# A retention layer and a feed-forward layer on one core: when the weight forms are stored, when GpSimd scales a unit's q, and where the masks of the scores stand

## The chip, the cores and the metric

The kernel runs on one core of a Trainium2 chip. The metric is the device time of one execution in microseconds. Three executions of the kernel before took 833.71, 831.45 and 833.17 us; the median is 833.17.

A core has five engines, each with an instruction order of its own: TensorE (PE; PEld is its loading of weights), VectorE (DVE), ScalarE (ACT), GpSimd (POOL) and SyncE (SP), which only issues DMAs. ScalarE and GpSimd issue DMAs too. Every engine works its instructions off in order: an instruction that waits holds up everything behind it on that engine.

## The reference

```python
def _attn_ref(q, k, v):                      # 8 x 8 x 576 x 64, float32
    scores = np.matmul(q, k.transpose(0, 1, 3, 2)) / np.sqrt(64)
    gamma = 1.0 - 2.0 ** (-5.0 - np.arange(H))
    rel = pos[:, None] - pos[None, :]
    Dmat = np.where(rel >= 0, gamma[:, None, None] ** rel[None, :, :], 0.0)
    return np.matmul(scores * Dmat[None], v)

def _moe_ref(x, w1, w2, w3, w_out):          # x: 4608 x 512
    a = x @ w1                               # 512 x 1024
    b = x @ w2                               # 512 x 1024
    h = a * b @ w3                           # 1024 x 1024
    return h @ w_out                         # 1024 x 512
```

The attention's output, with the heads laid side by side, is x (4608 tokens by 512). All is float32.

## The kernel before, in words

**Attention** runs in 20 units g: four pairs of batches, and in each pair five stretches of the sequence (64, 128, 128, 128 and 128 positions). A unit's q is scaled by a decay, its v by another; k and q are transposed; `score(g)` multiplies them (L233) into four PSUM banks and VectorE multiplies these by a mask into `pm` (L236, four instructions); `pv_state` and `pv` (L274, L299) make the output of the unit, which ScalarE copies to the token tiles `xT` (L306); `state` (L255) carries the sum over k and v to the next unit. In units 5 to 9 and from 12 on, q, and in some of these k, is loaded in blocks of 32 (`load_blocks`, L171, 16 DMAs for a tensor of 128 positions, on SP's queue), scaled on GpSimd for q (`scale_blocks`, L181, one instruction for each of the two batches) and transposed by VectorE (`front_blocks`, L190).

**Feed-forward.** The products are Strassen-Winograd products: seven block products P1 to P7 in place of eight, of weight forms (A11, A12, S3, A22, S1, S4, S2) with token forms (B11 and so on). W3 times W_out is multiplied first (w3o). An `up` step makes x times w1 and w2 for one of 12 tiles of 384 tokens and a quarter of the hidden columns (seven products, L528): VectorE adds five of them up in a tile `c` (`plus`, L533), ScalarE copies the sixth (L546, L561), and VectorE multiplies both halves of `c` into `ab` (L566). A `down` step takes pairs of 128-token tiles of `ab` through w3o (L651) to the output, with sums on VectorE (L614, L618, L620, L699, L701, L655).

**Two levels.** For the last eight token tiles, in four groups of two (`ready` says at which units a new group starts), `up2` steps make two levels of Strassen (L1068), 14 to a group, h = 0 and 1 with seven outer products each. Their weights are the outer forms of the weight forms. `weight_forms(h, second)` makes them in place in wA[h] and wS[h] with four sums, each of two VectorE instructions (L891), and stores each form in DRAM (`kept`); `next_forms` loads them from there one outer product at a time into a ring of three tiles `ra` (L969), issued on GpSimd. The stores of the first sum's results and of the parts that take no sum go out on GpSimd's queue; those of the other sums on SP's.

Inside a step of `up2`, GpSimd adds some of the tiles `cc` up (L1073), VectorE does it for results that come from PSUM (L1078, L1080). Completed results wait in a list; `multiply(n)` takes n off it and multiplies the two halves into `ab` (L1040, both inputs in SBUF). `finish()` runs what the last step left behind.

**The order around the change.** It is written out by hand. `todo` holds the steps to come; `work(n)` runs n of them and, after each, the small entries that follow it. `aside`, `spread`, `beside` and `loads` hold closures which the steps call at fixed places: each `plus` of an `up` step takes one from `aside` and one from `spread`. So an entry in `spread` that does nothing moves the next ones by one sum. `flush` runs all that is left in `spread`. In units 6 to 9 of the first loop, the `up` steps of token tile (1, 0) run between the attention units, with the weight forms spread between their sums: the first two `up` steps use wA[0], and after them the forms of h = 0 may overwrite it.

In the last loop `dealt` says how many steps each unit takes (3, 4, 4, 3, 3, 7, 7, 3, 7, 7 for units 10 to 19), and `tail` how many of them come after the transposes. A unit runs: the first steps, the scaling of the next unit's v and q, two steps with the transposes of q and k, the tail, `pv(g)`, the multiplications if a group ends, `state(g + 1)` and `score(g + 1)`, the next group's steps.

Of the kernel before, what the change touches and what calls it, by code (L numbers as in the profile page):

```python
# [13 lines left out]
ALU = mybir.AluOpType  # L14
# [5 lines left out]
def kernel(  # L20
# [20 lines left out]
    P = 128  # L41
# [16 lines left out]
    QC = CV // 2  # L58
# [64 lines left out]
    for c in (0, slice(1, NC)):  # L123
        n = short if c == 0 else P
# [11 lines left out]
    wA = [wp.tile([P, 2, 2, KD // 2, CV], F32, tag=f"wA{h}", name="wA") for h in halves]  # L136
# [35 lines left out]
                                      src[a, :, s0:s0 + BL, f * BL:(f + 1) * BL].rearrange("m r x -> r m x"))  # L172
        live["bl_" + nm, g] = t

    def scale_blocks(g):
        c = g % NC
        n, n0 = sizes[c] // BL, starts[c] // BL
        t = live["bl_q", g]
        for b in range(2):
            part = t[:, b * NP:(b + 1) * NP, :n, :]  # L180
            nc.gpsimd.tensor_tensor(  # L181
                out=part, in0=part, in1=gqs[:, :, n0:n0 + n].unsqueeze(3).to_broadcast([P, NP, n, BL]),
                op=ALU.mult)
# [388 lines left out]
    aside, owed, spread, beside, loads = [], [], [], [], []  # L572
    g = 0
# [306 lines left out]
    def weight_forms(h, second):  # L880

        engine = nc.sync if second else nc.gpsimd

        wa, ws = wA[h].rearrange("p r j c n -> p (r j) c n"), wS[h]

        def tt(out, in0, in1, op):
            def both():
                for w in (wa, ws):
                    o, x, y = (w[:, :, c, m * QC:(m + 1) * QC] if w is wa else w[:, :, m, :, c, :]
                               for m, c in (out, in0, in1))  # L890
                    nc.vector.tensor_tensor(out=o, in0=x, in1=y, op=op)  # L891
            return both

        def send(pieces):
            for lo, m, c in pieces:
                if m == 1 and c is not None and lo < 12 * P:
                    place = kept[h][:, :, 4 * P:8 * P].rearrange("a p (j c n) -> a p j c n", j=2, c=2)[:, :, :, c]
                    for a in range(4):
                        f, r = divmod(a, 2)
                        engine.dma_start(place[a], wA[h][:, r, :, c, m * QC + f * P:m * QC + f * P + P])  # L900
                    for j in range(2):
                        engine.dma_start(place[4:7, :, j].rearrange("a p n -> p a n"), wS[h][:, :, m, j, c, :])
                    continue
                n = 2 * P if c == 1 else 4 * P
                for a in range(4):
                    f, r = divmod(a, 2)
                    x = wA[h][:, r, :, :, m * QC + f * P:m * QC + f * P + P]
                    x = x.rearrange("p j c n -> p (j c) n") if c is None else x[:, :, c, :]
                    engine.dma_start(kept[h][a, :, lo:lo + n].rearrange("p (g n) -> p g n", n=P), x)
                to = kept[h][4:7, :, lo:lo + n].rearrange("a p n -> p a n")  # L910
                if c is None:
                    engine.dma_start(to, wS[h][:, :, m].rearrange("p a j c n -> p a (j c n)"))
                else:
                    for j in range(2):
                        engine.dma_start(to[:, :, j * P:(j + 1) * P], wS[h][:, :, m, j, c, :])

        if second:
            return [tt((1, 1), (1, 1), (1, 0), ALU.subtract), tt((0, 0), (1, 1), (0, 0), ALU.add),
                    tt((0, 1), (0, 1), (1, 1), ALU.subtract),
                    lambda: send([(8 * P, 0, None), (12 * P, 1, 1)])]  # L920
        return [tt((1, 0), (0, 0), (1, 0), ALU.subtract), lambda: send([(4 * P, 1, 0)]),
                lambda: send([(0, 0, None), (5 * P, 1, 1)])]

    def weight_of(slot, nm, w):
        lo = {"A11": 0, "A12": P, "S3": 4 * P, "A22": 5 * P, "S1": 8 * P, "S4": 9 * P, "S2": 12 * P}[nm]
# [212 lines left out]
    def add_group(gr):  # L1138
        X, Y = groups[gr]
        todo.extend((up2, gr, n) for n in range(14))  # L1140
        todo.extend([(down, (X, 0), (X, 1)), (down, (X, 2), (Y, 2)), (down, (Y, 0), (Y, 1))])

    def work(n):
        while n > 0 and todo:
            fn, *args = todo.pop(0)

            nxt = next((x for x in todo if x[0] in real), None)
            if nxt and nxt[0] is down:
                if fn is down:
                    args.append(nxt[1:])  # L1150
                else:
                    ahead(*nxt[1:], 1 if fn is up2 else 3)
            if g == G and not todo:
                fn(*args, last=True)
            else:
                fn(*args)
            n -= 1
            while todo and todo[0][0] not in real:
                todo.pop(0)[0]()
# [11 lines left out]
    for g in first_pair:  # L1171
        n = (1, 1, 2, 2)[g - NC]
        if not in_blocks[g + 2]:
            load(g + 2, "k")
            load_blocks(g + 2, "q")
        scale(g + 1, "v")
        if not in_blocks[g + 1]:
            front(g + 1, "k")
            front_blocks(g + 1, "q")
        half = (n + 1) // 2  # L1180
        if in_blocks[g + 1]:
            scale_blocks(g + 1)
            work(n - 1)
            aside.extend([lambda: front_blocks(g + 1, "q"), lambda: None, lambda: front_blocks(g + 1, "k")])
            work(1)
            while aside:
                aside.pop(0)()
            half = 0
        if in_blocks[g + 2] and g + 2 < 2 * NC:
            load_blocks(g + 2, "q")  # L1190
            load_blocks(g + 2, "k")
        work(half)
        if g < NC + 2:

            weight_forms(g - NC, False)[2]()
        pv(g)()
        load(g + 2, "v", nc.scalar if in_blocks[g + 2] else nc.sync)
        if in_blocks[g + 2] and (g + 2) % NC != NC - 1:
            load(g + 2, "k")
        state(g + 1)  # L1200
        score(g + 1)
        if not in_blocks[g + 2]:
            scale_blocks(g + 2)
        if g == NC + 1:
            list(strassen_tokens(1, 0))
            forms = [(lambda h=h, second=second: spread.extend(weight_forms(h, second)[:None if second else 2]),)
                     for h in halves for second in (False, True)]
            ups = [(up, 1, 0, fp) for fp in range(NQ)]
            later = (lambda: spread.append(lambda: None),)
            todo.extend([*ups[:2], forms[0], later, forms[1], ups[2], ups[3], (flush,), forms[2], (flush,), (down, (1, 0), (1, 1)),  # L1210
                         (down, (2, 2), (3, 2)), (open_second,), (down, (3, 0), (3, 1))])
        if not in_blocks[g + 1]:
            work(n // 2)
# [27 lines left out]
    for g in range(2 * NC, G):  # L1241
        n = dealt[g - 2 * NC]
        if g + 1 < G:
            q_blocks = g > 2 * NC
            if not q_blocks:
                beside.extend(lambda j=j: scale(g + 1, "q", range(j, j + H // 2)) for j in (0, H // 2))
            tail = {3: 0, 4: 1, 7: 3}[n]
            work(n - 2 - tail)
            beside.extend(lambda j=j: scale(g + 1, "v", range(j, j + H // 2)) for j in (0, H // 2))
            if q_blocks:  # L1250
                scale_blocks(g + 1)
            for nm in "qk":
                blocks_in = q_blocks if nm == "q" else g + 1 not in whole
                if blocks_in:
                    aside.append(lambda nm=nm: front_blocks(g + 1, nm))
                work(1)
                while aside:
                    aside.pop(0)()
                if not blocks_in and nm == "k":
                    while loads:  # L1260
                        loads.pop(0)()
                    front(g + 1, "k" if q_blocks else "kq")
                if g + 2 < G and not (nm == "k" and g + 2 in whole):
                    load_blocks(g + 2, nm)
            work(tail)
            for left in (loads, beside):
                while left:
                    left.pop(0)()
        else:
            work(n)  # L1270
        pv(g)()
        if g in ready:
            finish()
            multiply()
        if g + 2 < G:
            load(g + 2, "v", nc.gpsimd)
            if (g + 2) % NC != NC - 1:
                loads.append(lambda g=g: load(g + 2, "k", nc.gpsimd))
        if g + 1 < G:
            state(g + 1)  # L1280
            score(g + 1)
        if g in ready:
            add_group(ready[g])
            token_forms(ready[g])
    g = G
# [44 lines left out]
```

## Time and profile before

The profile was taken of the execution of 833.71 us. Its span, from the first to the last instruction, is 832.0 us, so 1.71 us lie around it.

| | us |
|---|---|
| time, median of three executions | 833.17 |
| time of the profiled execution | 833.71 |
| its span | 832.0 |
| TensorE's waits at 0 to 80 us of the span | 8.0 |
| TensorE's busy time from 80 to 304 us | 223.6 of 224 |
| TensorE's busy time from 304 to 320 us | 13.94 of 16 |
| TensorE's busy time from 320 to 816 us | 493.1 of 496 |
| VectorE's 64 multiplications L1040, median and longest of one | 0.549 and 3.267 |
| stores of weight forms on GpSimd's queue: wA in 256 KB, wA in 128 KB, wS in 768 KB, wS in 192 KB | 8, 16, 2 and 8 DMAs |

A timeline line of the profile has the start and the length in us, the engine, the line of the kernel, the operation, what it writes and reads, the shape, how many instructions were merged, and in brackets how long the engine idled before and what ended that. SPq, ACTq and POOL with DMA_DIRECT2D are DMAs being issued. A line of a table of stretches has the stretch, its length, busy time and number of instructions, the granted clock of TensorE (1.00 is full speed), the busy share of the DMA engines and GB/s.

### The profile page before, as it was taken

To read this page: it belongs to the slowest core of one execution; us is meant where nothing else is said; L and a number is where in the kernel's file an instruction comes from. 1 tells how busy PE (TensorE), PEld (TensorE's weight loads), DVE (VectorE), ACT (ScalarE), POOL (GpSimd) and SP (SyncE) were. 2 spreads that over 40 slices of the span, in tenths; PEclk is the share of its full clock that TensorE was granted. 3 is DMA by queue.
4 is the path that set the end of the run, shared out by engine and by line. 5 is a ranking of instruction groups with operands and counts; after the bars stand their busy time and mean duration, and the time that the engine had idled before them with its cause. 6 is when DMAs were issued, how large, how long until landed. Compare 5 with 4: busy or idle time off the path is not lost.

```text
span 832.0 us, 15840 instructions
## 1 busy us (share of the span) xinstructions
PE 815.6 (98%) x6117; PEld 735.6 (88%) x6117; DVE 546.6 (66%) x962; ACT 291.6 (35%) x609; POOL 233.6 (28%) x272
## 2 busy tenths in 40 slices
PE   7899999999999999999999999999999999999998
PEld 7889999744888998889999889998889998899987
DVE  4899999992553576754557655677745667646653
ACT  4787566581111111245443024341034331033300
POOL 1000000001506342125556005565006460045600
PEclk9999999999999999999999999999999999999999
DMA  9995464446347659667886447978245453046401
GB/s 191 228 224 133 78 152 128 120 109 110 137 79 218 124 115 267 212 181 202 195 227 186 97 86 208 237 224 220 54 94 180 158 196 115 35 149 213 142 26 51
DMA packets 197036, 126.96 MB, mean 153 GB/s; under 512 B 158072, under 2 KB 178680, under 8 KB 196960
## 3 DMA queue, kind: packets, MB, share of 16 engines
q1 hardware_dynamic: 168560, 50.40, 29.6%
q0 software_dynamic: 12704, 65.67, 24.3%
q10 hardware_dynamic: 15696, 9.87, 4.5%
q8 instruction: 48, 0.79, 0.4%
q14 instruction: 28, 0.23, 0.1%
HBM read 103.62 MB, written 22.28 MB: 151 GB/s over the span
## 4 chain that ended last, share of the span: by engine, by line
PE 88%; DVE 5%; DMA 3%; issue 1%; SPq 1%; ACT 1%; ACTq 0%; DVEq 0%
PE po L651 25%; PE up L1068 17%; PE up L528 15%; PE seed L1068 13%; PE ps L477 7%; PE xps L299 4%; PE sc L233 3%; PE xps L274 2%; PE st L255 1%; DMA ld_q<-in_q_dram 1%; PE tp L218 1%; SPq L171 1%; DVE ab L1040 1%; DMA gk<-decay_k_dram 1%; DVE pm L236 1%
## 5 line engine op out<-in xcount | busy, mean ns | idle before, releaser
L651 PE MATMUL po<-w3o,ab 128*128 128x256 f32 x552 | 124.8, 381 | 1.9 <-DVE pm L236 0.8
L651 PEld LDWEIGHTS po<-w3o,ab 128*128 128x128 f32 x552 | 103.8, 190 | 17.9 <-DVE ot L655 1.7
L1073 POOL TENSOR_TENSOR cc<-cc 128x384 f32<-128x384 f32 x112 | 109.6, 1003 | 3.6 <-ACT cc L1091 2.4
L1080 DVE TENSOR_TENSOR cc<-seed,cc 128x384 f32<-128x384 f32 x88 | 48.6, 552 | 69.1 <-PE seed L1068 60.2
L181 POOL TENSOR_TENSOR bl_q<-bl_q,gqs 128x512 f32<-128x512 f32 (+1 forms) x26 | 27.1, 1059 | 185.2 <-DMA bl_q<-in_q_dram 183.1
L1068 PE MATMUL up<-xT,ra 128*128 128x192 f32 x384 | 73.6, 328 | 0.1
L528 PE MATMUL up<-xT,wA 128*128 128x192 f32 x384 | 70.7, 328 | 0.2 <-DVE xT L496 0.2
L1080 DVE TENSOR_TENSOR cc<-up,cc 128x384 f32<-128x384 f32 x88 | 48.4, 550 | 29.8 <-PE up L1068 22.6
L533 DVE TENSOR_TENSOR c<-up,c 128x384 f32<-128x384 f32 x80 | 44.0, 551 | 35.7 <-PE up L528 34.5
L236 DVE TENSOR_TENSOR pm<-sc,mask 128x512 f32<-128x512 f32 (+1 forms) x80 | 45.3, 626 | 32.0 <-PE sc L233 31.9
L651 PE MATMUL po<-wB,forms 128*128 128x256 f32 x288 | 65.1, 379 | 0.0
L1068 PEld LDWEIGHTS up<-xT,ra 128*128 128x128 f32 x384 | 63.8, 190 | 1.3 <-PE tp L218 0.4
L528 PEld LDWEIGHTS up<-xT,wA 128*128 128x128 f32 x384 | 63.4, 190 | 1.6 <-issue 0.5
L969 POOL DMA_DIRECT2D ra<-kept x54 | 30.5, 565 | 117.0 <-PE seed L1068 96.0
L651 PEld LDWEIGHTS po<-wB,forms 128*128 128x128 f32 x288 | 54.7, 190 | 7.4
L1087 ACT COPY seed<-up 128x384 f32<-128x384 f32 x56 | 25.9, 463 | 100.6 <-PE up L1068 57.0
L477 PE MATMUL ps<-wo,w3T 128*128 128x512 f32 x128 | 55.1, 592 | 0.0
L1068 PE MATMUL up<-ra 128*128 128x192 f32 x288 | 54.7, 326 | 0.0
L477 PEld LDWEIGHTS ps<-wo,w3T 128*128 128x128 f32 x128 | 24.3, 190 | 30.1 <-issue 29.9
L1068 PE MATMUL seed<-e,ra 128*128 128x192 f32 x256 | 50.9, 329 | 0.0
L1068 PEld LDWEIGHTS up<-ra 128*128 128x128 f32 x288 | 48.1, 190 | 0.1
L528 PE MATMUL up<-T,wS 128*128 128x192 f32 x256 | 46.8, 326 | 1.2 <-DVE wS L149 1.2
(136 smaller groups left out, 1483.7 us busy)
## 6 DMA issues: line engine op xcount, KB each, us to landing
ra<-kept POOLq DMA_DIRECT2D x54, 896.0 KB, 5.0
raw<-in_moe_w_dram SPq DMA_DIRECT2D x72, 128.0 KB, 3.0
bl_q<-in_q_dram SPq DMA_DIRECT2D x192, 32.0 KB, 3.3
out_dram<-ot ACTq DMA_DIRECT2D x41, 128.0 KB, 2.2
bl_k<-in_k_dram SPq DMA_DIRECT2D x136, 32.0 KB, 2.9
raw<-in_moe_w_dram SPq DMA_DIRECT2D x16, 256.0 KB, 6.0
ld_k<-in_k_dram SPq DMA_DIRECT2D x8, 512.0 KB, 6.1
raw<-in_moe_w_out_dram SPq DMA_DIRECT2D x32, 128.0 KB, 2.7
```

The costliest lines, as they stand in the source:

```text
L181: nc.gpsimd.tensor_tensor(out=part, in0=part, in1=gqs[:, :, n0:n0 + n].unsqueeze(3).to_broadcast([P, NP, n, BL]), op=ALU.mult)
L236: nc.vector.tensor_mul(pm[:sz, b, j, :, :sz], sc[j][:sz, :, :sz], mask[:sz, :sz].unsqueeze(1).to_broadcast([sz, NP, sz]))
L299: nc.tensor.matmul(banks[r][heads[half], b, n, :sz], vs[:sz, b * H + 2 * p + j, :], pm[:sz, b, j, p, :sz], start=(c == 0 and m == 0), stop ...
L477: nc.tensor.matmul(ps, live["w3T", ft][:, g, :], live["wo"][:, g, :], start=(g == 0), stop=(g == KF - 1))
L528: nc.tensor.matmul(ps[:, w, :], a[:, w, r, :], b[:, r, :], start=(new and w == r == 0), stop=(w == r == 1), skip_group_check=True)
L533: nc.vector.tensor_add(c[:, to], ps, c[:, sb])
L651: nc.tensor.matmul(ps[nm], a[A][:, f, :], live["W"][B][:, f, :], start=(f == 0 and not on), stop=(f == NP - 1), skip_group_check=True)
L969: engine.dma_start(ring[n % 3], kept[n % 14 // 7][nm])
L1068: nc.tensor.matmul(ps[:, w, :], weight_of(slot, a, w), B[b], start=(new and w == 0), stop=True, skip_group_check=True)
L1073: nc.gpsimd.tensor_tensor(out=o, in0=o, in1=i, op=ALU.add)
L1080: nc.vector.tensor_add(c[:, j], ps, with_add[:, j])
L1087: nc.scalar.copy(p6, p1)
```

## The change

Three things change.

1. In `weight_forms` the store of the parts m = 1 is one store of the whole (`(4 * P, 1, None)`: four DMAs of 256 KB and one of 768 KB), after the first sum of the half. Before, it was two: the part with c = 1, which takes no sum at this point, went out with the parts m = 0 in units 5 and 6, the part with c = 0 after the sum. The branch of `send` for the two is gone. In the list of steps the third `up` step comes ahead of the entry that puts empty entries into `spread`, there are two empty entries instead of one, and the second forms of h = 0 follow them, so they are spread over the sums of the fourth `up` step alone.
2. `scale_blocks` takes the batches to scale. In the last loop, batch 0 is scaled one step earlier, batch 1 where both were.
3. Where a group ends, `multiply(2)` runs where all multiplications ran, and the rest after the scores of the next unit.

```diff
-    def scale_blocks(g):
+    def scale_blocks(g, batches=range(2)):
...
-        for b in range(2):
+        for b in batches:
...
         def send(pieces):
             for lo, m, c in pieces:
-                if m == 1 and c is not None and lo < 12 * P:
-                    place = kept[h][:, :, 4 * P:8 * P].rearrange("a p (j c n) -> a p j c n", j=2, c=2)[:, :, :, c]
-                    for a in range(4):
-                        f, r = divmod(a, 2)
-                        engine.dma_start(place[a], wA[h][:, r, :, c, m * QC + f * P:m * QC + f * P + P])
-                    for j in range(2):
-                        engine.dma_start(place[4:7, :, j].rearrange("a p n -> p a n"), wS[h][:, :, m, j, c, :])
-                    continue
                 n = 2 * P if c == 1 else 4 * P
...
-        return [tt((1, 0), (0, 0), (1, 0), ALU.subtract), lambda: send([(4 * P, 1, 0)]),
-                lambda: send([(0, 0, None), (5 * P, 1, 1)])]
+        return [tt((1, 0), (0, 0), (1, 0), ALU.subtract), lambda: send([(4 * P, 1, None)]),
+                lambda: send([(0, 0, None)])]
...
-            later = (lambda: spread.append(lambda: None),)
-            todo.extend([*ups[:2], forms[0], later, forms[1], ups[2], ups[3], (flush,), forms[2], (flush,), (down, (1, 0), (1, 1)),
+
+            later = (lambda: spread.extend([lambda: None] * 2),)
+            todo.extend([*ups[:2], forms[0], ups[2], later, forms[1], ups[3], (flush,), forms[2], (flush,), (down, (1, 0), (1, 1)),
...
-            work(n - 2 - tail)
+            work(n - 3 - tail)
+            if q_blocks:
+                scale_blocks(g + 1, (0,))
+            work(1)
             beside.extend(lambda j=j: scale(g + 1, "v", range(j, j + H // 2)) for j in (0, H // 2))
             if q_blocks:
-                scale_blocks(g + 1)
+                scale_blocks(g + 1, (1,))
...
         if g in ready:
             finish()
-            multiply()
+            multiply(2)
...
             state(g + 1)
             score(g + 1)
         if g in ready:
+
+            multiply()
             add_group(ready[g])
```

## The prediction

> **What bounds the kernel now.** I read the busy times first, then the chain of waits, then TensorE's own waits, then the stretches where it loses time, and there the other engines in order of time.
>
> ```profile
> PE 815.6 (98%) x6117; PEld 735.6 (88%) x6117; DVE 546.6 (66%) x962; ACT 291.6 (35%) x609; POOL 233.6 (28%) x272
> ...
> PE 88%; DVE 5%; DMA 3%; issue 1%; SPq 1%; ACT 1%; ACTq 0%; DVEq 0%
> ```
>
> TensorE is busy for 815.6 of 832.0 us and holds 88% of the chain. The change touches no matmul, so it can win only where TensorE waits, or where it runs slowly. The waits of TensorE that lie in the reach of the change are three: 2.06 us at 313.84, 0.84 at 550.14, 0.84 at 577.11. Table of stretches, TensorE's busy time and granted clock:
>
> ```profile
> 304.00:310.00 6.00, 6.00 (x39) 1.00 0.69 199
> 310.00:312.00 2.00, 1.77 (x11) 1.00 0.00 0
> 312.00:314.00 2.00, 0.16 (x1) 0.96 0.70 211
> 314.00:316.00 2.00, 2.00 (x7) 0.50 1.15 352
> 316.00:318.00 2.00, 2.00 (x37) 0.69 1.06 397
> ```
>
> The third column is the clock: after the gap TensorE works at 0.50 and 0.69 for some 3 us, so the gap costs more than its length. The cause, in order of time:
>
> ```profile
> 307.42 0.94 DVE L566 TENSOR_TENSOR ab<-c 128x768 f32<-128x768 f32 x1
> 308.97 0.56 DVE L533 TENSOR_TENSOR c<-up,c 128x384 f32<-128x384 f32 x1 [0.60 <-ACT c L546]
> 309.44 1.23 DVE L190 STREAM_TRANSPOSE qT<-bl_q 128x1024 f32<-128x1024 f32 x1
> 310.60 1.18 DVE L891 TENSOR_TENSOR wA<-wA 128x1024 f32<-128x1024 f32 x1
> 311.70 0.95 DVE L891 TENSOR_TENSOR wS<-wS 128x768 f32<-128x768 f32 x1
> 312.57 1.21 DVE L533 TENSOR_TENSOR c<-up,c 128x384 f32<-128x384 f32 x2
> 313.84 2.93 PE L528 MATMUL up<-xT,wS 128*128 128x192 f32 x8 [2.06 <-DVE c L533]
> ```
>
> The last product of the fourth `up` step (S4 B22) adds onto the bank of S1 T1, and must wait until VectorE's third sum (the second of the x2) has read it. VectorE is late because the weight-form sums (L891, 1.2 + 0.95 us a sum) stand in its order between the step's own sums.
>
> ```profile
> 543.64 2.06 POOL L181 TENSOR_TENSOR bl_q<-bl_q,gqs 128x512 f32<-128x512 f32 x2
> 544.53 4.16 DVE L1040 TENSOR_TENSOR ab<-cc 128x384 f32<-128x384 f32 x2
> 546.30 1.96 POOL L1073 TENSOR_TENSOR cc<-cc 128x384 f32<-128x384 f32 x2
> ...
> 571.78 4.67 DVE L1040 TENSOR_TENSOR ab<-cc 128x384 f32<-128x384 f32 x4
> 573.01 2.08 POOL L181 TENSOR_TENSOR bl_q<-bl_q,gqs 128x512 f32<-128x512 f32 x2
> ```
>
> A multiplication L1040 takes 0.55 us (median of 64). Here two take 1.58 and 2.65, and one takes 3.27, each ending about 0.43 us after a pair or a part of GpSimd's tensor work ends. Sums from PSUM are not slowed by the same GpSimd work (L1078, 1.02 us for two at 561.57, under L1073). TensorE's waits at 550.14 and 577.11 follow: a late sum, and a late mask.
>
> **Part 1: the stores and the sums of the weight forms.** GpSimd issues 2 x 5 + 2 x 5 stores instead of 2 x (5 + 6) + 2 x 6, 14 fewer at 0.72 to 0.76 us each, 10 us; none of it counts, as GpSimd idles there (14.00 us ahead of 297.31, 12.79 ahead of 320.26). What counts is VectorE's order. The third `up` step keeps one L891 pair (298.05) and loses two (302.87, 305.42); the fourth has them after its third sum. Worked out from the rows: the third step's fifth sum starts when its product ends, 304.0 instead of 304.95; L566 ends 1.62 later (as 279.77 to 281.39), at 305.6; ScalarE's copy at 306.2. The fourth step's first sum then follows its product, 306.6 to 307.2; qT to 308.4; second sum to 308.9; third sum when S1 T1 ends (309.17), done at 309.8. S4 B22 is due at 310.31 + 1.30 = 311.61, so it does not wait, with 1.8 us to spare. From there, with undisturbed spacings (1.39 and 1.03 as from 287.37, 1.90 and 1.98 as from 317.98): xps 313.00 and 314.03, scores 315.93, the down step at 317.91 instead of 321.86. **Gain 3.95 us** (2.23 of gap, 1.72 of slow clock).
>
> Where the sums go: kT (its load landed at 309.30) to 310.9, then in turn the first L891 pair to 313.0, fourth sum 313.5, L614, second pair to 316.1, fifth sum, L618 to 317.2, third pair to 319.2, L566, the second half's pair to 322.2, L620, masks from 322.8, the first done at 323.4. Late next is the down step's S1 product: it needs L620 and the bank that the first mask frees, and is due at 317.91 + 4 x 1.73 = 324.83. Spare: 1.4 us.
>
> The new wait: the first pair now overwrites what the last five stores read, issued at 303.03 to 306.7. The 768 KB store goes out at 305.95; landing took at most 4.3 us for these stores at 214 to 222, 6.3 at 260 to 268, 8.2 at 318 to 324. It lands at 310.3, 312.3 or 314.2; its sum is due at 312.05. The wait is 0, 0.2 or 2.1, less the spare 0, 0 or 0.7 on TensorE. I take 0: the DMA engines' share before 310 is 0.69, and nothing moves from 310 to 312. Queued behind the sum are the fourth sum, L618 and the masks. For the second half the stores go out at 321.2 to 325, and the sums come at 334.60 - 3.95 = 330.65. A landing of 8.2 puts them back 0.8; behind them VectorE idled 3.88 us for TensorE ahead of L699, so 0 (one for one beyond that cover).
> SP's eleven stores wait for the third pair and go out at 319 instead of 311.81. Behind them stand ld_k, ld_q twice, ld_k and the first ra load (328.38), 7 to 8 us later. ld_q is used at 355.11, ld_k at 361.65, ra at 366: covered by over 10 us.
>
> **Part 2: the halves of the scaling, and the masks.** At 534 to 567 the first half runs at 538.3, where GpSimd idled 2.84 us; its load had been issued by 524. The second half ends at 544.7 instead of 545.71, so the first L1040 ends at 545.1 and the second at 545.6, ahead of L1073. The matmuls at 550.14 start at 548.50 + 0.73 = 549.23: **gain 0.91**. At 571.78, two L1040 stand ahead of the masks instead of four, and GpSimd's first half comes at 572.46. VectorE's second L1040 ends at 573.95, or, if it is held until the second half is done, at 575.5. The first mask ends at 574.6 or 576.1; TensorE wants it at 574.27 + 1.73 = 576.00: **gain 1.11** or 1.0.
> In the other units the earlier half lies ahead of masks only, which read PSUM: 0. At 455 the first half waits for its load until 456.75 and holds up one ra load (454.89) by 2.7 us; that weight is used after 498: 0. The masks there were not waited for: 0.
>
> **Sum.** 3.95 + 0.91 + 1.11 = 5.97, so the execution of 833.71 us (span 832.0, and 1.71 around it) becomes 827.7. The median of the runs, 833.17, is 0.54 lower; it becomes **827.2**.
>
> The row first: a gap of 2.06 us was followed by a granted clock of 0.50. The Trainium skill, TensorE: Matmul & The Clock Gate (Why this matters for your kernels), warns of idle gaps over about 3 us. By that rule this gap would cost its length alone, and the sum would be 4.2 us instead of 6.0.
> The row at 572.25: an L1040 shown to start 0.76 us before L181 still lasted to 575.52. The Trainium skill, SBUF — State Buffer (Who interferes with whom), says that such a pair is held by the instruction that issues first. By that rule and the shown starts the multiplication would have gone first, splitting the scaling would not help at 571.78, and the sum would be 4.9 us.
>
> **Rivals.**
> A, part 1 alone works: L1040 is held as long as before because another GpSimd instruction fills the time. For it: 545.71 to 548.26 is full of GpSimd work. Against it: 1.6 us lie between the halves' new end and L1073. 833.17 - 3.95 = 829.2.
> B, the gap only moves: the third sum is early, but stores or kT land 2 us or more after the spare and TensorE waits for a mask at 324.8, with the slow clock after it. For it: 8.2 us landings at 318. Against it: idle DMA engines at 310. 833.17 - 2.02 = 831.2, no change within what can be told.
> C, slower: the same wait of VectorE for the 768 KB store, grown. Each us past the spare is one us of TensorE, plus 1.72 of slow clock. It eats all 5.97 from a landing at 312.05 + 1.4 + 4.25 = 317.7, 11.8 us after issue. At 15 us: 833.17 - 5.97 + 7.5 + 1.72 = 836.4. Against it: 8.2 is the longest row.
>
> **Chances.** Forecast 0.63 (0.02 of it better still), A 0.17, B 0.13, C 0.07. A measurement of this kernel can tell about 0.3%, 2.5 us. Faster 0.80, same 0.13, slower 0.07. The range goes from 825.4 (the sum, less 1.8 for the spread of the runs, 831.45 to 833.71) to 831.3 (B).
>
> **What would show it.** No wait of TensorE at 311 to 314 and a clock of 1.00 through 318; L891 pairs after the third sum; down step near 317.9; L1040 never above 2.2 us; no waits near 549 and 576. Wrong if VectorE idles ahead of L891 for DMA by over 1.4 us, or if TensorE gets a new wait of over 1 us between 311 and 345.

## The result, and the profile after

22 executions of each kernel: the changed one takes 830.14 us in the median (828.74 to 832.30), the one before 834.08 (831.45 to 839.16). The ratio is 0.9951, 95% interval 0.994 to 0.9962, so 4.1 us less (3.2 to 5.0). The sum was 5.97 us, outside this interval. The time lies within the range, 2.9 us above the 827.2 named; 0.9 of that is the kernel before, whose median was 833.17 in the three executions shown first. By the time alone rival A, with 3.97 us, fits better than the sum; the profile and the runs below decide between them.

The profiled execution of the changed kernel took 832.11 us, with a span of 830.4. The first 234 us, up to the 64x64 scores, which no part of the change reaches, took 1.65 us longer than in the profile before. Below, stretches between the same two instructions are compared, not points of the span.

Page of the changed kernel, busy times and chain of waits:

```profile
PE 817.5 (98%) x6117; PEld 737.2 (89%) x6117; DVE 543.2 (65%) x962; ACT 291.8 (35%) x609; POOL 223.0 (27%) x258
...
PE 86%; DVE 5%; DMA 4%; issue 2%; SPq 2%; ACT 1%; POOL 0%; ACTq 0%; DVEq 0%; POOLq 0%
```

GpSimd has 14 instructions fewer. TensorE is the bound as before. Table of stretches of the changed kernel (stretch, length and TensorE's busy time, granted clock, share of the DMA engines, GB/s):

```profile
304.00:310.00 6.00, 6.00 (x38) 1.00 0.78 225
310.00:312.00 2.00, 2.00 (x15) 1.00 1.06 396
312.00:314.00 2.00, 2.00 (x14) 1.00 0.23 48
314.00:316.00 2.00, 2.00 (x43) 1.00 0.01 4
316.00:318.00 2.00, 2.00 (x38) 1.00 0.03 8
```

The gap and the slow clock are gone. But the DMA engines are full from 310 to 312 (share 1.06); in the profile before the same place, 1.65 us earlier, has a share of 0.34. VectorE of the changed kernel, in order of time:

```profile
310.85 0.56 DVE L533 TENSOR_TENSOR c<-up,c 128x384 f32<-128x384 f32 x1 [0.38 <-PE up L528]
313.99 1.25 DVE L190 STREAM_TRANSPOSE kT<-bl_k 128x1024 f32<-128x1024 f32 x1 [2.58 <-DMA bl_k<-in_k_dram]
315.16 1.18 DVE L891 TENSOR_TENSOR wA<-wA 128x1024 f32<-128x1024 f32 x1
...
326.14 0.68 DVE L620 TENSOR_TENSOR forms<-forms,ab 128x512 f32<-128x512 f32 x1
326.74 2.47 DVE L236 TENSOR_TENSOR pm<-sc,mask 128x512 f32<-128x512 f32 x4
```

The third sum is done at 311.4, in time for S4 B22. Then VectorE stands 2.58 us for k's last blocks ahead of kT. Everything behind it in VectorE's order is late: the sums of the weight forms, L620, and the masks. TensorE pays for that. The down step, first of the profile before, then of the changed kernel:

```profile
321.86 5.45 PE L651 MATMUL po<-w3o,ab 128*128 128x256 f32 x24
327.15 3.62 PE L651 MATMUL po<-wB,forms 128*128 128x256 f32 x16
330.60 1.89 PE L651 MATMUL po<-wB,ab 128*128 128x256 f32 x8
332.33 1.89 PE L651 MATMUL po<-w3o,ab 128*128 128x256 f32 x8
334.15 1.10 PE L274 MATMUL xps<-qT,sb 64*64 64x128 f32 x32
```

```profile
319.56 5.45 PE L651 MATMUL po<-w3o,ab 128*128 128x256 f32 x24
324.85 1.89 PE L651 MATMUL po<-wB,forms 128*128 128x256 f32 x8
327.48 1.99 PE L651 MATMUL po<-wB,forms 128*128 128x256 f32 x8 [0.74 <-DVE pm L236]
329.31 1.89 PE L651 MATMUL po<-wB,ab 128*128 128x256 f32 x8
331.60 1.99 PE L651 MATMUL po<-w3o,ab 128*128 128x256 f32 x8 [0.40 <-DVE ot L655]
333.52 1.10 PE L274 MATMUL xps<-qT,sb 64*64 64x128 f32 x32
```

With undisturbed spacings the last product L651 would start near 329.9 (the down step, from its first product to the next `pv_state`, takes 12.29 us in the profile before and 13.96 here): 1.67 us are given back.

Parts 2 and 3, VectorE and then GpSimd of the changed kernel (L1032 is L1040 of before, the multiplication):

```profile
543.85 1.10 DVE L1032 TENSOR_TENSOR ab<-cc 128x384 f32<-128x384 f32 x2
...
570.73 2.87 DVE L1032 TENSOR_TENSOR ab<-cc 128x384 f32<-128x384 f32 x2
573.52 2.47 DVE L236 TENSOR_TENSOR pm<-sc,mask 128x512 f32<-128x512 f32 x4
575.91 1.01 DVE L1032 TENSOR_TENSOR ab<-cc 128x384 f32<-128x384 f32 x2
```

```profile
543.00 1.05 POOL L181 TENSOR_TENSOR bl_q<-bl_q,gqs 128x512 f32<-128x512 f32 x1
...
571.42 1.07 POOL L181 TENSOR_TENSOR bl_q<-bl_q,gqs 128x512 f32<-128x512 f32 x1
...
573.03 1.47 POOL L181 TENSOR_TENSOR bl_q<-bl_q,gqs 128x512 f32<-128x512 f32 x1
```

The two multiplications at 544 take 1.10 us instead of 4.16. At 571 two, not four, stand ahead of the masks, and the masks start in time. One by one, the first of the two takes 2.40 us, until the first half of the scaling is done, and the second 0.55; there it is the second half of the scaling that is held up (1.47 us instead of 1.05). TensorE's waits of 0.84 us at 550 and at 577 are gone. There are two small new ones for `ra`: 0.45 us at 547.78 and 0.27 at 634.79.

### The profile page after: what moved, and what is told of

It is laid out like the page before. It is cut to its first block, busy times and chain, and to the rows that moved or that the text cites. A ratio compares the mean times of both kernels' runs of the same rounds, so it can differ in the third digit from the quotient of the medians.

```text
span 830.4 us, 15815 instructions
## 1 busy us (share of the span) xinstructions
PE 817.5 (98%) x6117; PEld 737.2 (89%) x6117; DVE 543.2 (65%) x962; ACT 291.8 (35%) x609; POOL 223.0 (27%) x258
## 4 chain that ended last, share of the span: by engine, by line
PE 86%; DVE 5%; DMA 4%; issue 2%; SPq 2%; ACT 1%; POOL 0%; ACTq 0%; DVEq 0%; POOLq 0%
PE po L651 24%; PE up L1060 16%; PE up L528 15%; PE seed L1060 12%; PE ps L477 7%; PE xps L299 3%; PE sc L233 3%; DMA ra<-kept 2%; DMA bl_k<-in_k_dram 2%; PE xps L274 2%; SPq L171 2%; PE tp L218 2%; PE st L255 1%; DVE pm L236 1%; PE idle L131 1%
## 5 line engine op out<-in xcount | busy, mean ns | idle before, releaser
L651 PE MATMUL po<-w3o,ab 128*128 128x256 f32 x552 | 124.6, 381 | 1.5 <-DVE ot L655 1.0
L651 PEld LDWEIGHTS po<-w3o,ab 128*128 128x128 f32 x552 | 103.8, 190 | 17.5 <-DVE ot L655 2.5
L651 PE MATMUL po<-wB,forms 128*128 128x256 f32 x288 | 65.4, 379 | 0.7 <-DVE pm L236 0.7
L651 PEld LDWEIGHTS po<-wB,forms 128*128 128x128 f32 x288 | 54.6, 190 | 8.5 <-DVE pm L236 1.1
```

Source lines behind the costliest of these rows:

```text
L651: nc.tensor.matmul(ps[nm], a[A][:, f, :], live["W"][B][:, f, :], start=(f == 0 and not on), stop=(f == NP - 1), skip_group_check=True)
```

## Experiments

All times are medians (of 6 to 12 executions where nothing else is said), all ratios are against the kernel before, run beside it.

| kernel | median us | ratio | 95% interval |
|---|---|---|---|
| part 1 alone | 832.04 | 0.9973 | 0.996 to 0.9987 |
| parts 2 and 3 alone | 833.12 | 0.9988 | 0.9973 to 1.0002 |
| changed, split stores | 830.56 | 0.995 | 0.9932 to 0.9968 |
| changed, first sum of h = 1 behind the masks | 834.58 | 1.0005 | 0.9991 to 1.002 |
| changed, once more | 830.66 | 0.9949 | 0.9929 to 0.9968 |
| changed, split stores, once more | 829.86 | 0.9941 | 0.9923 to 0.9959 |
| changed, kT one sum later | 829.70 | 0.9942 | 0.9919 to 0.9965 |
| before, gap filled | 835.78 | 1.0017 | 1.0003 to 1.0032 |
| changed, split stores, another kT later | 829.95 | 0.995 | 0.9933 to 0.9967 |
| whole stores alone, two executions | 843.66 | 1.0113 | 1.0079 to 1.0146 |
| part 2 alone, one execution | 832.55 | | |
| part 3 alone, one execution | 834.98 | | |

Steps of 1 us lie within these intervals, so the profiles carry most of what follows. Two stretches of TensorE's timeline, start to start, us. A runs from the 64x64 scores (at 233.89 in the profile before) to `pv_state` behind the fourth up step (316.70 before), B from there over the down step to the next `pv_state` (334.15 before):

| profile | A | B |
|---|---|---|
| before | 82.81 | 17.45 |
| parts 2 and 3 alone | 81.26 | 17.20 |
| part 2 alone | 81.96 | 17.20 |
| part 3 alone | 83.58 | 17.20 |
| changed, split stores (three profiles) | 80.70, 79.23, 80.64 | 17.20 |
| changed | 79.11 | 18.87 |
| changed, once more | 79.43 | 18.90 |
| part 1 alone | 79.48 | 18.84 |
| changed, kT one sum later | 79.77 | 17.20 |

### Part 1, and parts 2 and 3

Against the changed kernel, part 1 alone:

```diff
-            work(n - 3 - tail)
-            if q_blocks:
-                scale_blocks(g + 1, (0,))
-            work(1)
+            work(n - 2 - tail)
...
-                scale_blocks(g + 1, (1,))
+                scale_blocks(g + 1)
...
-            multiply(2)
+            multiply()
...
-
-            multiply()
```

> Part 1 alone (the whole store of the parts m = 1, and the new order of the steps); the scaling and the multiplications as before. Theory G (the gap before S4 B22 goes, 3.94 us, but the load of k in blocks lands late, VectorE stands at kT, the masks come late, and 1.57 us are given back at 324 to 332): 2.3 us faster than before, no TensorE wait at 311 to 314, a wait of 0.5 to 1.2 us for a mask before the down step's fourth product. Rival (the wait for the mask was chance of the one profiled run): 3.9 us faster, no wait for a mask.

2.25 us faster, with the waits of the changed kernel: 0.71 us for a mask at 327.60, 0.40 for L655 at 331.72, and the old waits of 0.84 and 0.85 at 549.22 and 576.18. Theory G holds; the rival of 3.9 us lies outside the interval (1.1 to 3.3). So does that of rival A in the prediction, by which part 1 alone would be the whole gain.

> Parts 2 and 3 alone; stores and order of the steps as before. Theory: 2.0 us faster than before (0.91 at 550, 1.11 at 577), the gap of 2.06 us at 311 to 314 and its slow clock stay. Rival (the moved scaling holds up loads of ra on GpSimd's queue, as the two new waits of 0.27 and 0.5 us for ra in the changed kernel's profile may say): 0.9 to 1.0 us faster, with waits for ra at 547 and 635.

1.0 us faster (2.3 faster to 0.2 slower). Both waits at 550 and 577 are gone and the gap at 313 stays. There is a wait of 0.20 for `ra` at 548.02, none at 635. The time does not tell the theory (2.0) from the rival (0.9 to 1.0); the profile speaks for the theory. Part of the gain may be hidden: these executions lose 2.6 us in the mean to a slow clock, those of the kernel before run beside them 1.5, and in the profile the slow clock lies near 15 and 42 us, where the change does not reach. The profile shows something else, too. After a gap of 1.74 us the clock was not lowered (stretches of parts 2 and 3 alone, third column):

```profile
314.00:316.00 2.00, 0.42 (x2) 1.00 0.85 256
316.00:318.00 2.00, 2.00 (x40) 1.00 1.14 359
```

### Which of the two does what: part 2 and part 3 each alone

> Part 2 alone (the halves of the scaling). Theory: the wait at 550 (0.84 us) is gone, the gap at 313 stays; at 577 four L1040 stand ahead of the masks again, two of them free of GpSimd's work, so 0.3 to 0.9 us of the wait stay. Rival (splitting alone cures both): no wait at 577.

> Part 3 alone (two multiplications ahead of the masks, the rest behind). Theory: the wait at 550 (0.84 us) stays; at 577 two L1040 stand ahead of the masks, the second held up by the whole scaling (2.08 us), so the wait falls from 0.84 to 0 to 0.3 us. Rival (the scaling alone made the masks late): the wait at 577 stays within 0.2 us of 0.84.

Part 2 alone: no wait at 550, 0.91 us at 577, the whole of it. Part 3 alone: 0.84 at 550, none at 577. VectorE of part 2 alone, then of part 3 alone:

```profile
570.55 4.73 DVE L1040 TENSOR_TENSOR ab<-cc 128x384 f32<-128x384 f32 x4
```

```profile
573.92 3.73 DVE L1040 TENSOR_TENSOR ab<-cc 128x384 f32<-128x384 f32 x2
```

Split or whole, the scaling holds up L1040 where they meet: four with the two halves take 4.73 us, as long as with both together before (4.67). Splitting helps at 544, where the first half is moved out of reach; at 571, in these two runs, only the shorter queue ahead of the masks does. Each part cures one wait. Both have the stores of before. There the second half of the scaling holds up an L1040 (1.47 us) in all five profiles with the split scaling; in the four with whole stores it is held up itself, and the multiplication takes 0.55. Whether part 2 alone would have cured the wait at 577 beside whole stores was not run.

### What makes k late: the stores

The changed kernel with the stores of before; the branch of `send` for the halves is back, too:

```diff
-        return [tt((1, 0), (0, 0), (1, 0), ALU.subtract), lambda: send([(4 * P, 1, None)]),
-                lambda: send([(0, 0, None)])]
+        return [tt((1, 0), (0, 0), (1, 0), ALU.subtract), lambda: send([(4 * P, 1, 0)]),
+                lambda: send([(0, 0, None), (5 * P, 1, 1)])]
```

> The changed kernel with the stores of before (split parts m = 1, the half c = 1 sent in units 5 and 6). Theory S (the whole stores, 1.75 MB in five DMAs at 304 to 308, delay the load of k and the first sum of the second forms): kT starts before 312, the masks are in time, 1.6 us faster than the changed kernel, 5.6 faster than before. Rival Q (k lands late for its own queue on SyncE, whose issues took 13.4 and 9.4 us instead of 11.8 and 8.1): kT near 314 again, as the changed kernel, 4.1 faster than before.

> The changed kernel with the split stores of before once more, beside the changed kernel. Theory S: no wait for a mask or for L655 at 324 to 332, the last blocks of k land within 4 us; the place between the down step's first and last product is 1.2 to 1.6 us shorter; 1.0 to 1.5 us faster than the changed kernel. Rival: the same time within 0.5 us, if something else pays for it.

DMA issues in the half microsecond to a microsecond in which k's last blocks go out, of the changed kernel and of the one with split stores (last figure: us to landing):

```profile
kept<-wS POOLq DMA_DIRECT2D x1, 768.0 KB, 6.1
bl_k<-in_k_dram SPq DMA_DIRECT2D x3, 32.0 KB, 5.7
```

```profile
kept<-wS POOLq DMA_DIRECT2D x1, 192.0 KB, 3.6
bl_k<-in_k_dram SPq DMA_DIRECT2D x2, 32.0 KB, 3.9
```

In the profile before they land in 2.9 us. The last block but one lands 4.7 to 5.5 us after its issue in the six profiles with whole stores, 2.7 to 3.9 in the eight with split ones. SyncE's queue is not late: it begins these 16 loads 221.6 to 222.1 us after the same product near 78 us in the profiles of before, the changed kernel, part 1 alone, and parts 2 and 3 alone. Only the issues themselves take longer, 8.4 to 9.7 us with whole stores and 8.1 to 8.8 with split ones. VectorE with split stores, second profile:

```profile
312.69 1.25 DVE L190 STREAM_TRANSPOSE kT<-bl_k 128x1024 f32<-128x1024 f32 x1 [0.25 <-DMA bl_k<-in_k_dram]
...
324.83 0.69 DVE L620 TENSOR_TENSOR forms<-forms,ab 128x512 f32<-128x512 f32 x1
325.43 1.89 DVE L236 TENSOR_TENSOR pm<-sc,mask 128x512 f32<-128x512 f32 x3
```

kT waits 0.25 us instead of 2.58, stretch B is 17.20 in all three profiles, and no wait for a mask is left. Theory S holds for the stage. It does not hold for the time: the first of the two runs was 4.0 us faster than before, near rival Q's 4.1 and not the 5.6 expected, and the median of the second is only 0.8 us under that of the changed kernel run beside it, with intervals that overlap. Two of the three profiles show where the rest went: TensorE waits 1.37 and 1.31 us near 294 for `ld_k` (L255). Part 2 alone and part 3 alone, with the same stores, show it too, the longest in part 3 alone. TensorE of the profile before, then of part 3 alone:

```profile
291.59 1.10 PE L255 MATMUL st<-ld_v,ld_k 128*64 128x64 f32 x32
```

```profile
296.22 1.15 PE L255 MATMUL st<-ld_v,ld_k 128*64 128x64 f32 x32 [2.49 <-DMA ld_k<-in_k_dram]
```

With split stores the early half goes out in unit 6 (six DMAs, from 30.2 us after the 64x64 scores on), and SyncE issues this `ld_k` 52.8 to 53.8 us after the scores instead of 51.0 to 51.8. Ahead of it stand 16 loads of q: they begin 30.6 us after the scores in every profile, and are issued by 44.8 to 45.8 us with split stores, by 43.0 to 43.8 with whole ones. `ld_k` is used at 57.7 and lands 4.6 to 6.4 after issue. Five of eight profiles with split stores have the wait (0.75 to 2.49 us), none of six with whole ones. So the whole stores cost 1.67 us in stretch B and save 0.9 on the mean in stretch A (7.14 us over eight profiles). That leaves 0.8 between the two kernels, as measured, though within the noise.

### kT one sum later

```diff
-            aside.extend([lambda: front_blocks(g + 1, "q"), lambda: None, lambda: front_blocks(g + 1, "k")])
+            kT = [lambda: front_blocks(g + 1, "k")]
+            if g == NC + 3:
+                kT = [lambda: None, lambda: (front_blocks(g + 1, "k"), aside.pop(0)())]
+            aside.extend([lambda: front_blocks(g + 1, "q"), lambda: None, *kT])
```

> The changed kernel with kT's transposition one sum later in the fourth up step, behind the first sum of the second forms. Theory S: VectorE stops standing for kT and stands instead for the 768 KB store ahead of the L891 of wS, 0.8 to 1.3 us; masks 1.0 to 1.4 us earlier; the wait of 0.74 us for a mask goes; 0.7 to 1.3 us faster than the changed kernel. Rival (the 768 KB store lands no earlier than k): the wait only changes its name, and the time is that of the changed kernel within 0.3 us.

```profile
312.54 1.22 DVE L891 TENSOR_TENSOR wA<-wA 128x1024 f32<-128x1024 f32 x1
314.38 0.96 DVE L891 TENSOR_TENSOR wS<-wS 128x768 f32<-128x768 f32 x1 [0.62 <-DMA kept<-wS]
...
315.72 1.24 DVE L190 STREAM_TRANSPOSE kT<-bl_k 128x1024 f32<-128x1024 f32 x1
...
325.99 2.48 DVE L236 TENSOR_TENSOR pm<-sc,mask 128x512 f32<-128x512 f32 x4
```

VectorE of this kernel stands 0.62 us for the 768 KB store and not at all for k. Stretch B is 17.20, no wait for a mask, and the early `ld_k` stays. The time is 0.96 us under that of the changed kernel run beside it, as theory S says, but the intervals overlap. By the profile this is the best form of part 1 with whole stores: A and B together are 96.97 us, against 97.98 and 98.33 for the changed kernel. With split stores they are 97.90, 96.43 and 97.84.

### Other ways to make the masks early

```diff
-            todo.extend([*ups[:2], forms[0], ups[2], later, forms[1], ups[3], (flush,), forms[2], (flush,), (down, (1, 0), (1, 1)),
+            todo.extend([*ups[:2], forms[0], ups[2], later, forms[1], ups[3], (flush,), forms[2], (down, (1, 0), (1, 1)),
```

> The changed kernel without the second emptying of the list ahead of the down step: the first sum of h = 1 (two L891, 2.08 us) comes after the masks, between the sums of the down step. Theory G: the masks are 2.0 us earlier and TensorE's wait of 0.74 us for a mask and the late L655 after it go, 1.0 to 1.5 us faster than the changed kernel. Rival (the masks are not what counts, the sums of the down step are late next): as the changed kernel within 0.3 us, with the wait at L655 near 331 grown.

A miss: 0.5% slower than the changed kernel (1.0005 against 0.9951). The wait for a mask does go, but GpSimd's stores of h = 1 go out at 330.44 instead of 325.64 and land after 7.3 to 9.2 us. VectorE, then TensorE, of this kernel:

```profile
340.78 1.23 DVE L891 TENSOR_TENSOR wA<-wA 128x1024 f32<-128x1024 f32 x1 [6.32 <-DMA kept<-wA]
...
346.93 1.22 DVE L891 TENSOR_TENSOR wA<-wA 128x1024 f32<-128x1024 f32 x1
...
348.93 0.95 DVE L655 TENSOR_TENSOR spare<-po,spare 128x256 f32<-128x256 f32 x2
```

```profile
349.40 3.52 PE L651 MATMUL po<-w3o,carry 128*128 128x256 f32 x8 [1.92 <-DVE spare L655]
```

The next sums of h = 1 stand 6.32 us for these stores, the third pair comes ahead of L655, and TensorE waits 1.92 us for that; the clock is 0.50 in the 2 us that follow. This is rival C's mechanism at the other half: more cover was eaten than VectorE's 3.88 us.

### The whole stores without the new order

```diff
-            later = (lambda: spread.extend([lambda: None] * 2),)
-            todo.extend([*ups[:2], forms[0], ups[2], later, forms[1], ups[3], (flush,), forms[2], (flush,), (down, (1, 0), (1, 1)),
+            later = (lambda: spread.append(lambda: None),)
+            todo.extend([*ups[:2], forms[0], later, forms[1], ups[2], ups[3], (flush,), forms[2], (flush,), (down, (1, 0), (1, 1)),
```

The scaling and the multiplications are those of before, too.

> Of part 1 only the whole stores; the order of the steps, the scaling and the multiplications as before. Theory: the first sum of the second forms, in the third up step near 302 to 304, now overwrites what the whole stores read (issued from 303 on, landed 4.3 us later for 256 KB, 5.3 to 6.1 for 768 KB), so VectorE stands 5 to 10 us in that step, TensorE with it for 4 to 9 us: 837 to 844 us. The new order of steps is what makes the whole stores possible. Rival (the stores are out early enough, as the down step covers it): within 1 us of before.

VectorE, then TensorE, of this kernel:

```profile
310.25 1.23 DVE L891 TENSOR_TENSOR wA<-wA 128x1024 f32<-128x1024 f32 x1 [6.60 <-DMA kept<-wA]
312.26 0.96 DVE L891 TENSOR_TENSOR wS<-wS 128x768 f32<-128x768 f32 x1 [0.78 <-DMA kept<-wS]
```

```profile
317.17 2.93 PE L528 MATMUL up<-xT,wA 128*128 128x192 f32 x8 [6.06 <-ACT c L546]
...
322.02 1.57 PE L528 MATMUL up<-xT,wS 128*128 128x192 f32 x8 [1.92 <-DVE c L533]
```

As expected, in two executions. The new order of the steps is not only what takes the gap away; without it the whole stores cost some 10 us. Part of that is a slow clock that begins in the first of these waits and lasts 6.83 us, and a wait of 1.46 us for L655 at 357.66.

### The clock after the gap

```diff
+        if (i, n, fp) == (1, 0, NQ - 1):
+            keep_busy(8)
         product(p5, "S4", "B22")
```

> The kernel before with eight products of no use (ident x ident, 1.9 us at full clock) put into the gap ahead of S4 B22; nothing else changes. Theory (the gap is followed by a slow clock, at least in some executions, and that costs 0.7 us or more in the mean): the work after the gap starts at the same place, the clock is 1.00 from 312 to 318, and the mean time is 0.7 to 1.7 us under that of before. Rival (the gap costs its length alone): the same time as before within 0.5 us, and as many executions under a full mean clock as before.

A miss that settles little. The clock was 1.00 from 312 to 318, but the kernel was slower than before. This profile has a new wait of 1.46 us for L655 at 351.00. The products take a PSUM bank, which may change the order in which the banks behind them change hands; but the whole stores alone have the same wait at the same place without such products, so its cause is not shown. What the slow clock costs is better read from the executions: of 71 of the kernel before, 33 show a mean granted clock of 1.00, and the mean of (1 - clock) x span is 1.34 us; of 32 of the changed kernel it is 20, and 0.88 us. The difference, 0.46 us, has a standard error of 0.3, and the mean takes in slow stretches anywhere in the span.

### A kT in the third group of down steps

```diff
                 if blocks_in:
+                    if (g, nm) == (2 * NC + 4, "k"):
+                        aside.append(lambda: None)
                     aside.append(lambda nm=nm: front_blocks(g + 1, nm))
```

> The changed kernel with the split stores of before, and kT of unit 15 one sum later in the third down step near 606, behind the sum that TensorE waits for there (0.57 us in every profile so far). Theory: no wait near 608, the down step at 318 takes 12.3 us; 1.5 to 2.2 us faster than the changed kernel, 5 to 6 faster than before. Rival (the wait at 608 goes on to the next sum): as with the split stores alone, 4.2 to 5 faster than before.

The edit missed its place: the kT at 605 has 1024 columns, a unit of 128 positions, while unit 15 has 64, and its transposition comes later. The wait of 0.57 us stood at 606.97 as before. The run is a third sample of the split stores and no more.

## Why the prediction was right, and where it was off

**What bounds the kernel**: right. Only TensorE's waits and its clock counted; TensorE holds 86% of the chain, 88% before. 10 us less of GpSimd's work shows in no time.

**Part 1, the gap**: right to the hundredth where the profile is compared with the profile. The down step was to start at 317.91; it starts at 319.56, less the 1.65 us lost before the change begins: 317.91. But 1.72 of the 3.95 us were slow clock, and that term was mis-sized. It was taken from the one execution profiled. In three other profiles with the old order the gap is 1.74, 1.14 and 1.49 us and the clock stays at 1.00; over the executions the changed kernel loses 0.46 us less to the clock (1.34 - 0.88, with a standard error of 0.3), not 1.72. The gap itself was the longest of the four, too.

**Part 1, the step that failed**: "kT (its load landed at 309.30) to 310.9". The landing was taken over from the profile before, although five whole stores were to go out just then. The prediction counted them against the sums that overwrite what they read, and there gave a landing of 310.3 to 314.2; it did not count them against a load under way on the same DMA engines. k's last blocks took 5.5 to 5.8 us instead of 2.9 to 3.0, kT ended 2.7 us later than worked out (315.24 - 1.65 against 310.9), more than the spare of 1.4, and 1.67 us were lost. This is rival B in half: the gap did move in part, to the mask named there, without a slow clock after it.

**What was not seen at all**: the early half of the split stores delays `ld_k` near 294. The profile before has no wait there (its load landed 0.3 us ahead of its use), five of eight profiles with these stores do. So part of the agreement is luck: 0.9 us that nobody forecast makes up for half of the 1.67 us lost.

**The waits behind the stores**: right. The sums of h = 1 were to be put back 0.8 us with no cost; VectorE waits 0.79 us at 335.98 and TensorE none. The kernel with h = 1's first sum behind the masks shows what happens when the cover is gone.

**Part 2** (0.91) and **part 3** (1.11 or 1.0): right. The waits of 0.84 and 0.84 to 0.91 us go, one by each part. In the changed kernel's profile 0.99 and 1.11 us are gained at the two places, and 0.6 lost to the wait for `ra` just before the first. One sign failed: an L1040 was never to take over 2.2 us, and the first of the two at 571 takes 2.40. The second does not wait, so the pair ends at 573.59, which is 574.65 in the time of the profile before, between the 573.95 and the 575.5 foreseen.

**The two pages.** By the Trainium skill, TensorE: Matmul & The Clock Gate (Why this matters for your kernels), gaps over about 3 us are to be avoided; read as a threshold, shorter ones cost their length alone. The rows differ: the gap of 1.92 us at 349.40 was followed by a clock of 0.50. A sum of 4.2 us by that rule was near the 4.1 measured, but for another reason, since 1.67 us were lost elsewhere. By SBUF — State Buffer (Who interferes with whom), the instruction that issues first should hold the pair. Part 2 alone shows the first of four L1040 under way 0.69 us before the first half of the scaling (570.55 against 571.24), and the four still took 4.73 us. That speaks against counting on the order of the shown starts at this place. So does the second half of the scaling: it starts 0.02 to 0.03 us ahead of the multiplication in all nine profiles with the split scaling, and yet five times the multiplication is held up and four times the scaling. The prediction's 4.9 us took off the whole 1.11, but most of that comes from part 3: part 3 alone has no wait at 577.

**The sum by the profiles**: stretches A and B together are 99.67 us in the mean of the four profiles with the old order and stores, and 98.21 in the three with part 1: 1.46. The waits at 550 and 577 make 0.84 and 0.84. That is 3.1, against 4.1 (3.2 to 5.0) measured. It lies at the edge of the interval, and the rest is not placed; the time of the same product near 78 us alone spreads over 77.4 to 80.0 us in the profiles.

**Open**: seven of nine profiles with the split scaling show waits for `ra`, of 0.20 to 1.19 us in all, at changing places; none of five without it does. The load issued near 541 lands in 5.1 to 7.3 us with it and 5.1 to 6.8 without. Whether the split causes these waits was not settled.

## What to carry to other kernels

A store that is made larger competes with the loads under way at that moment: before a landing time is taken over from the profile before, look at what the change issues in the few microseconds around it. When an order is tuned, a wait and its neighbours are one thing: in the profiles with the old order the gap at 313 is 2.06 and 1.74 us where there is no wait for `ld_k` ahead of it, 1.14 and 1.49 us where there is one. It looks as if VectorE catches up while TensorE waits; then a remedy for one wait can lengthen the other. A term that rests on one execution's granted clock should be weighed by how many executions show it.

## What the runs showed of the hardware that was not expected

The length of a gap did not decide whether the granted clock falls after it. It fell after gaps of 1.84, 1.86, 1.92, 2.06 and 2.40 us, and did not after 1.74, 1.80 and, in part 3 alone at 296.22, after 2.49 us. Two gaps of 1.92 us went either way: at 349.40 in one kernel with a slow clock after it, at 322.02 in another without (there the clock, slow since the gap before, came back to 1.00 at 320.74, within the gap). A slow stretch has a clock of 0.50 and lasts 3.41 us in these traces, in three of them 6.83 or 10.24.

A multiplication on VectorE with both inputs in SBUF can be held by GpSimd's tensor work for about the whole of it, split or not: 4.67 us for four under 2.08 us of scaling, 4.73 under two halves, 1.96 for four at 791.50 in a profile with no GpSimd work beside them. It can go the other way: where the second half of the scaling meets a multiplication, five profiles have 1.06 us for the scaling and 1.47 for the multiplication, the four with whole stores 1.47 and 0.55, with the same 0.02 to 0.03 us between the starts. What decides it was not found.
